# First-batch attention scores as one full-float32 product, and the last short unit's first layer moved between the last tile's layers

## Chip, cores and metric

The kernel runs on one core of a Trainium2 chip. The metric is the device time of one execution in microseconds; for the kernel before, three runs gave 1084.39 us in the median (1082.83 to 1085.16). One further execution was recorded by the hardware profiler; all rows of the trace below are from that one.

## The reference

Causal attention with a decay, over 8 batches of 8 heads (576 positions, 64 wide), then a two-layer feed-forward network (512 to 2048 to 512) over the 4608 rows that it gives. Cut to what matters:

```python
scores = (q @ k.T) / sqrt(64)                       # q, k: (8, 8, 576, 64) float32
cum    = cumsum(log(clip(f, 1e-4, 1)), axis=-1)
scores = where(causal, -1e9, scores + cum[:, None] - cum[None, :])
attn   = softmax(scores)
x      = (attn @ v) -> (4608, 512)
h      = x @ w_in
g      = h * clip(h + 3, 0, 6) / 6
out    = g @ w_out
```

## The kernel before, in words

**Attention, by visits.** The list `VH` (line 97) holds 68 visits. The first batch is cut in another way than the rest: four visits of kind A, each with the first 256 positions of a pair of heads, and eight of kind B, each with the other 320 queries of one head against all 576 keys. Then come 56 visits of kind F, one for each head of the batches 1 to 7. A and B go through `scores` (line 542), which makes scores with the keys on the partitions, so that their exponentials are the weights of the product with v; F goes through `rows` (line 592), which is left as it is apart from its tiles.

**How a product of q and k is made exact.** `load_x` brings q and k of a visit into a tile ST (q on partitions 0 to 63, k on 64 to 127). `parts` (line 442, on GpSimd) rounds them to the reduced type float32r into TQ and TK. `rests` (line 450) copies these rounded parts by two DMAs within the chip into the halves of two further tiles, T7 and T1, and has GpSimd subtract them from ST, so that T7 and T1 also hold what the rounding left. In `group` (line 547) two matmuls then add up in PSUM: line 549 multiplies the rounded parts (with rows for the decay and for the row's maximum, 97 partitions in all), line 550 the mixed products (128 partitions). A third, of float16 and 128 or 64 columns (line 552), adds the causal mask where a block lies on the diagonal. A visit A has four groups (256, 128, 256, 128 columns), a visit B five (320, 320, 320, 192, 64).

**The maximum.** Before that, `natural` (line 475) makes the same scores roughly, from the rounded parts alone, with the queries on the partitions; VectorE takes each row's maximum (line 491); `max_rows` (line 496) turns the maxima by a matmul (line 500), and a DMA of SyncE (line 503) lays them as row 96 of TQ. The names of this chain in the profile are `pn`, `MC`, `ptm` and `mr`.

**Buffers.** TQ and TK have three buffers (visit v uses v mod 3), T1 and T7 two, ST three. So `parts` of a visit waits until the `scores` three visits before have read TK and TQ; `load_x` waits until `rests` has read ST; and the DMAs of `rests` wait until the `scores` two visits before have read T1 and T7.

**Weights.** w_in and w_out come as 64-bit floats, in 32 pieces of 512 KB. Each is loaded (line 238) into one of a few slots, turned into float32 by one instruction of ScalarE and two of VectorE (lines 251 to 253), squared on ScalarE for its scale (line 257), and split in two float16 halves (`w_split`, lines 284 to 295: for most of w_in by two matmuls, lines 287 and 288; for the last quarter of w_in and all of w_out by VectorE, line 295). `W_RATE` hands out eight such steps in a visit A, two in a visit B and four in a visit F.

**The network, as filler.** Once a batch's rows are there, `moe_tile` works off 512 of them: 16 first-layer units (`h_unit`, line 768, matmuls of lines 775 to 777, then ScalarE, VectorE, ScalarE, VectorE into gT) and four second-layer units (`out_unit`, line 815, 48 matmuls of 512 columns each, lines 819 to 821, into a PSUM tile `po`, one eviction by ScalarE, line 825, one DMA). The 64 rows of a batch that are left over go pairwise through `moe_short` (line 848): four `h_short` units (48 matmuls of 128 columns each, lines 797 to 799, into `phs`) and one `out_unit`. These units are generators; `fill` (line 917) puts pieces of them between the steps of the visits. The PSUM tiles of these units come from `mm_tile` (line 761): every third from `ps_t` (one buffer), the others from `ps_m` (two buffers).

**Order.** A scheduler then orders each engine's instructions by its own estimate of when each can start. Each engine and SyncE's queue of DMAs runs its instructions strictly in that order.

**The end.** After the last visit nothing is left but the last tile and the last short unit: first layer of the tile, its second layer, first layer of the short unit (whose result goes into the first 128 columns of gT, which the second layer has read by then), second layer of the short unit.

Of the kernel before, what the change touches and what calls it, by code (L numbers as in the profile page):

```python
# [20 lines left out]
def kernel(  # L21
# [87 lines left out]
    TQ = [cpool.tile([97, SP], F32R, name=f"TQ{i}") for i in range(NQK)]  # L109
    TK = [cpool.tile([97, SP], F32R, name=f"TK{i}") for i in range(NQK)]  # L110
    T1 = [cpool.tile([P, SP], F32R, name=f"T1{i}") for i in range(NL)]
    T7 = [cpool.tile([P, S], F32R, name=f"T7{i}") for i in range(NL)]
# [5 lines left out]
    def init_qk(i, eng):  # L118
        eng.memset(TQ[i].bitcast(F32)[64:96, :], 0.0)
        eng.memset(TQ[i].bitcast(F32)[64:66, :], 1.0)  # L120
        eng.memset(TK[i].bitcast(F32)[64:96, :], -1.0)
        eng.memset(TK[i].bitcast(F32)[96:97, :], 1.0)
        eng.memset(TK[i].bitcast(F32)[:, S:], 0.0)

# [289 lines left out]
    def load_c(v):  # L414
        kind, n = VH[v]
        t = TK[v % NQK].bitcast(F32)[D:D + 2]
# [9 lines left out]
        else:  # L426
# [4 lines left out]
            if PIN0:  # L431
                small.append(d.ins)

# [16 lines left out]
    def rests(v):  # L450
        i, j = v % NQK, v % NL
        s = ST[v % NST]
# [43 lines left out]
    def max_rows(v):  # L496
        i = v % NQK
# [5 lines left out]
        d = nc.sync.dma_start(TQ[i].bitcast(F32)[96:97, 0:m * P], mr.bitcast(F32)[:m])  # L503
# [38 lines left out]
    def scores(v):  # L542

        i, j = v % NQK, v % NL
        ph = p2.tile([P, 1600], F32, tag="PHL", name=f"pf_{v}")

        def group(dst, k0, q0, q1, m):
            ks = slice(k0, k0 + P)
            nc.tensor.matmul(dst, TK[i][0:97, ks], TQ[i][0:97, q0:q1], start=True, stop=False)
            nc.tensor.matmul(dst, T1[j][:, ks], T7[j][:, q0:q1], start=False, stop=(m == 0))  # L550
# [238 lines left out]
    def h_short(u, j):  # L789
# [20 lines left out]
        g = [gT[:, i, n * j:n * j + n, 0:P] for i in range(2)]  # L810
# [4 lines left out]
    def out_unit(s, three, col, rows_):  # L815
        po = mm_tile(f"po_{rows_[0]}", three)
        ts_ = slice(s * P, (s + 1) * P)
        for fc in range(NFC):
            nc.tensor.matmul(po, gT[:, 0, fc, ts_], w2[:, fc, 0, :], start=(fc == 0), stop=False)  # L819
            nc.tensor.matmul(po, gT[:, 0, fc, ts_], w2[:, fc, 1, :], start=False, stop=False)  # L820
            nc.tensor.matmul(po, gT[:, 1, fc, ts_], w2[:, fc, 0, :], start=False, stop=(fc == NFC - 1))  # L821
            if fc % 2 and fc < NFC - 1:
                yield 2.0 - H_COST
# [7 lines left out]
    def moe_tile(t, c0=0, c1=TT):  # L831
# [10 lines left out]
        if c0 == 0:  # L842
            moe_scale_out(t)
# [217 lines left out]
```

## Time and profile before

| | us |
|---|---|
| three runs, median (lowest to highest) | 1084.39 (1082.83 to 1085.16) |
| the profiled execution's own time | 1078.21 |
| its span, first to last instruction | 1076.4 |
| TensorE busy | 1012.2 (94% of the span), 7650 matmul records |
| VectorE busy | 731.5 (68%) |
| ScalarE busy | 587.9 (55%) |
| GpSimd busy | 407.8 (38%) |
| mean granted TensorE clock | 0.989 |

How to read the trace: PE is TensorE, DVE VectorE, ACT ScalarE, POOL GpSimd, SP SyncE (SPq its DMA queue). A matmul's record lasts from its start to the modelled end of its results, so records of a stream overlap; what one costs in a stream is the distance from its start to the next one's. A matmul with full float32 operands shows as two records, one with any other type as one. "Idle before, releaser" names what ended an engine's idle time.

### The profile page before, as it was taken

The page shows a single profiled execution, that of the slowest core. Times are in us where ns is not written, and L with a number is a line of the kernel's source. Part 1 is how long each engine was busy: PE and PEld are TensorE (multiplying, and loading weights), DVE is VectorE, ACT ScalarE, POOL GpSimd, SP SyncE. Part 2 cuts the span into 40 slices and gives each one's busy share as a digit, 9 for nine tenths or more (in the row PEclk, how much of TensorE's full clock was granted, in tenths as well). Part 3 has the DMA queues.
Part 4 walks back from the last instruction along what each step waited for, and adds up shares of the span by engine and source line. Part 5 has one row for each costly group of instructions (what it writes and reads, how often), then busy time and mean ns, then how long its engine had stood idle before and what let it go on. Part 6 is the DMA issues. An engine that isn't in the chain of part 4 may idle for free.

```text
span 1076.4 us, 21155 instructions
## 1 busy us (share of the span) xinstructions
PE 1012.2 (94%) x7650; PEld 600.5 (56%) x7650; DVE 731.5 (68%) x1903; ACT 587.9 (55%) x1189; POOL 407.8 (38%) x505
## 2 busy tenths in 40 slices
PE   2889987899999999999999999999999999999995
PEld 1557854665555755555555755555555755544453
DVE  7897999996885669866865677767855678305101
ACT  4787656765664557555654557555744567225102
POOL 7353455454433444443434344543442442000000
PEclk9989989999999999999999999999999999999999
DMA  7976548966656766567465476557565654300010
GB/s 241 288 212 191 135 100 149 201 146 128 156 101 137 138 151 129 114 148 162 97 127 109 104 167 128 127 133 170 106 110 113 118 96 86 70 30 1 1 40 10
DMA packets 259140, 133.78 MB, mean 124 GB/s; under 512 B 226933, under 2 KB 228525, under 8 KB 259037
## 3 DMA queue, kind: packets, MB, share of 16 engines
q1 hardware_dynamic: 259036, 132.44, 55.6%
q8 instruction: 60, 0.98, 0.4%
q14 instruction: 44, 0.35, 0.1%
HBM read 47.93 MB, written 9.73 MB: 54 GB/s over the span
## 4 chain that ended last, share of the span: by engine, by line
PE 65%; DVE 17%; ACT 6%; issue 5%; DMA 5%; SPq 1%; POOL 1%; ACTq 0%; DVEq 0%; POOLq 0%
PE po L819 10%; PE po L821 10%; PE po L820 10%; PE ph L775 7%; PE ph L776 6%; PE ph L777 6%; DVE pp L620 3%; PE pn L609 3%; PE pn L612 3%; ACT pp L632 2%; DVE ring L649 2%; DMA vst<-in_vS_dram 2%; DVE gT L786 2%; DVE r L784 1%; DVE nb L626 1%
## 5 line engine op out<-in xcount | busy, mean ns | idle before, releaser
L820 PE MATMUL po<-w,gT 128*128 128x512 f16 x576 | 215.7, 382 | 2.5 <-DVE w L295 2.5
L819 PE MATMUL po<-w,gT 128*128 128x512 f16 x576 | 213.6, 382 | 4.1 <-ACT gT L811 3.1
L821 PE MATMUL po<-w,gT 128*128 128x512 f16 x576 | 215.7, 382 | 0.1
L632 ACT ACTIVATE pp<-pp,nb 128x192 f32<-128x192 f32 x280 | 138.9, 552 | 134.8 <-DVE nb L626 134.2
L775 PE MATMUL ph<-xT,w 128*128 128x512 f16 (+1 forms) x576 | 200.2, 358 | 7.1 <-DVE r L784 6.9
L649 DVE TENSOR_TENSOR ring<-pp,ring 128x128 f16<-128x128 f32 (+2 forms) x216 | 144.5, 678 | 83.6 <-ACT ring L646 80.8
L776 PE MATMUL ph<-xT,w 128*128 128x512 f16 (+1 forms) x576 | 199.7, 357 | 0.0
L777 PE MATMUL ph<-xT,w 128*128 128x512 f16 (+1 forms) x576 | 199.2, 357 | 0.0
L447 POOL TENSOR_SCALAR TK<-ST 64x576 fp32r<-64x576 f32 (+1 forms) x68 | 50.1, 737 | 245.2 <-PE pn L609 202.5
L620 DVE CUSTOM_DVE_ANT_0 pp<-pn,W 128x192 f32<-128x192 f32 x280 | 123.3, 482 | 24.7 <-PE pn L612 22.5
L459 POOL TENSOR_TENSOR T<-ST,T 64x576 fp32r<-64x576 f32 (+1 forms) x68 | 99.7, 1466 | 82.8 <-DMA T<-TK 74.3
L609 PE MATMUL pn<-TK,TQ 68*128 68x192 f32 x336 | 124.4, 384 | 6.3 <-issue 5.2
L784 DVE SCALAR_TENSOR_TENSOR r<-r,ph 128x512 f32<-128x512 f32 (+1 forms) x144 | 89.1, 620 | 54.6 <-ACT r L781 54.2
L785 ACT CAST gT<-r 128x512 f16<-128x512 f32 (+1 forms) x144 | 81.5, 569 | 76.9 <-DVE r L784 76.2
L786 DVE TENSOR_TENSOR gT<-r,gT 128x512 f16<-128x512 f32 (+1 forms) x144 | 102.8, 717 | 20.6 <-ACT gT L785 19.0
L781 ACT ACTIVATE r<-ph,bias_r,SC 128x512 f32<-128x512 f32 (+1 forms) x144 | 103.6, 724 | 20.7 <-PE ph L777 17.5
L646 ACT CAST ring<-pp 128x192 f16<-128x192 f32 x280 | 114.3, 449 | 0.0
L612 PE MATMUL pn<-T,T 128*128 128x192 f32 x336 | 113.0, 363 | 0.0
L456 POOL TENSOR_TENSOR T<-ST,TQ 64x576 fp32r<-64x576 f32 (+2 forms) x68 | 100.2, 1474 | 14.2 <-PE pn L612 5.3
L821 PEld LDWEIGHTS <-gT 128*128 128x128 f16 x576 | 56.5, 99 | 71.1 <-issue 9.4
L820 PEld LDWEIGHTS <-gT 128*128 128x128 f16 x576 | 56.5, 99 | 63.4 <-issue 6.4
L655 POOL TENSOR_TENSOR ring<-pp,ring 128x128 f16<-128x128 f32 x96 | 59.9, 624 | 78.2 <-ACT ring L646 33.9
(146 smaller groups left out, 1958.0 us busy)
## 6 DMA issues: line engine op xcount, KB each, us to landing
ST<-in_qk_dram SPq DMA_DIRECT2D x64, 288.0 KB
T<-TK SPq DMA_DIRECT2D x64, 144.0 KB
out_dram<-o SPq DMA_DIRECT2D x33, 256.0 KB
ring<-in_w_out_dram SPq DMA_DIRECT2D x16, 512.0 KB
T<-TQ SPq DMA_DIRECT2D x56, 144.0 KB
vst<-in_vS_dram SPq DMA_DIRECT2D x7, 1040.0 KB
ring<-in_w_in_dram SPq DMA_DIRECT2D x9, 512.0 KB
w<-in_w_in_dram SPq DMA_DIRECT2D x7, 512.0 KB
```

The lines of the kernel that those rows point to most:

```text
L609: nc.tensor.matmul(dst, TQ[i][0:D + 4, qs], TK[i][0:D + 4, a:e], start=True, stop=False)
L612: nc.tensor.matmul(dst, T7[j][:, qs], T1[j][:, a:e], start=False, stop=True)
L620: nc.vector.tensor_tensor_reduce(pp[:r, w:w + kw], pn[:r, o:o + kw], W[:r, 4 * P + r - kw:4 * P + r], 1.0, -3.0e38, ALU.add, ALU.max, accu ...
L632: nc.scalar.activation(x_, x_, AF.Exp, bias=nb[:r, e0 + x:e0 + x + 1], scale=0.125)
L649: eng.tensor_tensor(hl[:r, a:a + c * P], pp[:r, at[c] + 64:at[c] + kw], hl[:r, h0[c] + 64:h0[c] + kw], op=ALU.subtract,)
L775: nc.tensor.matmul(ph, w1[0][:, cc, fs_], xh, start=(cc == 0), stop=False)
L776: nc.tensor.matmul(ph, w1[0][:, cc, fs_], xl, start=False, stop=False)
L777: nc.tensor.matmul(ph, w1[1][:, cc, fs_], xh, start=False, stop=(cc == NCC - 1))
L786: nc.vector.tensor_tensor(gT[:, 1, fc, c0:c1], r, gT[:, 0, fc, c0:c1], op=ALU.subtract)
L819: nc.tensor.matmul(po, gT[:, 0, fc, ts_], w2[:, fc, 0, :], start=(fc == 0), stop=False)
L820: nc.tensor.matmul(po, gT[:, 0, fc, ts_], w2[:, fc, 1, :], start=False, stop=False)
L821: nc.tensor.matmul(po, gT[:, 1, fc, ts_], w2[:, fc, 0, :], start=False, stop=(fc == NFC - 1))
```

## The change

Two independent edits.

**Scores of the visits A and B.** `group` issues one matmul with full float32 operands on 97 partitions in the place of the two float32r ones: `T1[...][0:97]` by `T7[...][0:97]`, which now hold k and q as they are. The mask's matmul stays. A new `load_raw` brings q and k for these two tiles straight from HBM (two DMAs a visit) and the decay rows a second time (`load_c(v, raw=True)`: one or two small DMAs); `rests` does only that for A and B, so the two copies within the chip and GpSimd's two subtractions are gone for these 12 visits. `init_raw` sets the constant rows of the two tiles once. The maxima go to row 96 of T7, no longer of TQ. `natural` and `parts` stay. TQ and TK are now only read by `natural` in these visits, and shrink to 68 partitions. T1 and T7 come from a pool of their own, since F takes them as float32r tiles.

**The end.** The last tile and the last short unit become one generator: first layer of the tile, then the short unit's four `h_short` units into a buffer of their own (`gs`, in the tile vst, which is free by then), then the tile's four second-layer units, then the short unit's second layer as two `out_unit`s of 256 columns each, with an eviction and two DMAs each.

```diff
     def rests(v):
+        if VH[v][0] != "F":
+            load_raw(v)
+            return
         i, j = v % NQK, v % NL
+        T1[j] = p_r.tile([P, SP], F32R, tag="T1", name=f"T1_{v}")
+        T7[j] = p_r.tile([P, S], F32R, tag="T7", name=f"T7_{v}")
...
+    def load_raw(v):
+        kind, n = VH[v]
+        nq, nk, q0 = spans(v)
+        load_c(v, raw=True)
+        for t, d, o, w in ((T7, 0, q0, nq), (T1, D, 0, nk)):
+            t = t[v % NL][0:D, 0:w]
+            if kind == "A":
+                nc.sync.dma_start(
+                    t.rearrange("p (h s) -> p h s", h=2),
+                    qk[2 * n:2 * n + 2, d:d + D, 0:QA].rearrange("h p s -> p h s"),
+                )
+            else:
+                nc.sync.dma_start(t, qk[n, d:d + D, o:o + w])
...
-        d = nc.sync.dma_start(TQ[i].bitcast(F32)[96:97, 0:m * P], mr.bitcast(F32)[:m])
+        d = nc.sync.dma_start(T7[v % NL][96:97, 0:m * P], mr.bitcast(F32)[:m])
...
         def group(dst, k0, q0, q1, m):
-            ks = slice(k0, k0 + P)
-            nc.tensor.matmul(dst, TK[i][0:97, ks], TQ[i][0:97, q0:q1], start=True, stop=False)
-            nc.tensor.matmul(dst, T1[j][:, ks], T7[j][:, q0:q1], start=False, stop=(m == 0))
+            nc.tensor.matmul(
+                dst, tk[0:97, k0:k0 + P], tq[0:97, q0:q1], start=True, stop=(m == 0)
+            )
...
+        last = t == B - 1
+        if last:
+            gs = vst.bitcast(F16).rearrange("p c e -> p (c e)")[:, 0:2 * NFC * P]
+            gs = gs.rearrange("p (a f t) -> p a f t", a=2, f=NFC)
+            for j in range(NG):
+                yield from h_short(t // 2, j, gs)
         r0 = t * S + (64 if t else 0)
         for s in range(c0 // P, c1 // P):
             yield from out_unit(s, t > 0 or s * P >= QA, UO + t, [r0 + s * P])
+        if last:
+            for cols in ((0, DM // 2), (DM // 2, DM)):
+                yield from out_unit(0, True, UX + t, [(t - 1) * S, t * S], gs, cols)
...
+    init_raw(0, nc.gpsimd)
+    rests(0)
...
-            if b % 2:
+            if b % 2 and b < B - 1:
                 queue(moe_short(b // 2), P)
```

**How the order moves, first place: SyncE's queue near its start.** The names are the destinations; `mr` is the row of maxima of a visit, `w` and `ring` are slots for weights, `Q` and `K` the new names of T7 and T1. Before, from the first visit's maxima to the second's:

```order
L503 DMA TQ_93<-mr_187 1x4x128
L355 DMA v_111<-in_vS_dram 128x3x520
L356 DMA xT_118<-in_vS_dram 128x520
L357 DMA xT_118<-in_vS_dram 64x520
L407 DMA ST_103<-in_qk_dram 128x2x256
L238 DMA ring_126<-in_w_in_dram 128x1024
L412 DMA ST_104<-in_qk_dram 128x576
L238 DMA w_115<-in_w_in_dram 128x1024
L422 DMA TK_96<-decay_dram 2x2x256
L454 DMA T_101<-TQ_95 64x512
L455 DMA T_99<-TK_98 64x512
L503 DMA TQ_94<-mr_246 1x4x128
```

Now, the same stretch and the row behind it:

```order
L525 DMA Q_104<-mr_196 1x4x128
L359 DMA v_114<-in_vS_dram 128x3x520
L360 DMA xT_121<-in_vS_dram 128x520
L361 DMA xT_121<-in_vS_dram 64x520
L416 DMA ST_108<-in_qk_dram 128x576
L422 DMA TK_97<-decay_dram 2x576
L416 DMA ST_106<-in_qk_dram 128x576
L525 DMA Q_105<-mr_244 1x4x128
L242 DMA w_118<-in_w_in_dram 128x1024
```

Two weight pieces and two copies within the chip no longer stand between the two visits' maxima; the next weight piece follows behind both.

**Second place: VectorE where the visits B end and the visits F begin.** `w_115` and `w_118` with line 295 or 299 are splits of w_out, `pp` is the first step of an F visit's softmax, `pp_0_1670` and `pp_0_1608` that of the first one. Before:

```order
L726 TENSOR_SCALAR rs_0_1642<-rs_0_1642,SC 128x3
L620 ISA pp_0_1670,MF_108<-pn_0_1661,W 128x192
L620 ISA MF_108 128x1
L620 ISA pp_0_1670,MF_108<-pn_0_1661,W 128x576
L620 ISA MF_108 128x1
L620 ISA pp_0_1670,MF_108<-pn_0_1661,W 64x64
L620 ISA MF_108 64x1
L387 COPY SC<-SC 64x1
L727 TENSOR_TENSOR xf_1640<-pav,rs_0_1642 128x3x64
L295 SCALAR_TENSOR_TENSOR w_115<-w_115,SC 128x512
```

Now:

```order
L299 SCALAR_TENSOR_TENSOR w_118<-w_118,SC 128x512
L757 TENSOR_TENSOR xhl_1410<-xf_1409,xhl_1410 128x3x128
L299 SCALAR_TENSOR_TENSOR w_118<-w_118,SC 128x512 x4
L745 TENSOR_SCALAR rs_0_1580<-pav 128x3
L748 RECIPROCAL rs_0_1580<-rs_0_1580 128x3
L750 TENSOR_SCALAR rs_0_1580<-rs_0_1580,SC 128x3
L751 TENSOR_TENSOR xf_1578<-pav,rs_0_1580 128x3x64
L299 SCALAR_TENSOR_TENSOR w_118<-w_118,SC 128x512 x4
L644 ISA pp_0_1608,MF_111<-pn_0_1599,W 128x192
```

Before, all 16 splits of w_out stand behind the first F visit's `pp`, spread over the first six F visits; now ten stand ahead of it and the other six behind it, before the second F visit's `pp`.

**Third place: TensorE at the very end.** Before, the short unit's first layer (`phs_3`) and its second layer (`po_12475`) meet so:

```order
L798 MATMUL phs_3_12420<-xS_120,w_113 128x128
L799 LDWEIGHTS w_114
L799 MATMUL phs_3_12420<-xS_120,w_114 128x128
L819 LDWEIGHTS gT
L819 MATMUL po_12475<-w_115,gT 128x512
```

Now the end of `phs_3` lies between the first 36 matmuls of the first half (`po_0_12523`) and the second half (`po_256_12576`), which is free to start without the last quarter of `gs`:

```order
L847 MATMUL po_0_12523<-w_118,vst 128x256
L821 LDWEIGHTS w_116
L821 MATMUL phs_3_12260<-xS_123,w_116 128x128
L822 LDWEIGHTS w_116
L822 MATMUL phs_3_12260<-xS_123,w_116 128x128
L823 LDWEIGHTS w_117
L823 MATMUL phs_3_12260<-xS_123,w_117 128x128
L845 LDWEIGHTS vst
L845 MATMUL po_256_12576<-w_118,vst 128x256
```

Behind `phs_3` there now come 25 matmuls of `po_256_12576` before the first that needs its result. By the count in `mm_tile`, `phs_0`, `phs_2`, `phs_3`, the tile's second and third second-layer units and both halves share the two buffers of `ps_m`; `phs_1` and the tile's first and fourth unit take the one of `ps_t`.

More of the change, by code (lines that the diff above doesn't have):

```diff
@@ L108 @@
     PIN_V = 1
[L109 to L112, printed above, removed]
+    TQ = [cpool.tile([D + 4, SP], F32R, name=f"TQ{i}") for i in range(NQK)]
+    TK = [cpool.tile([D + 4, SP], F32R, name=f"TK{i}") for i in range(NQK)]
+    p_r = ctx.enter_context(tc.tile_pool(name="p_r", bufs=NL))
+    T1 = [p_r.tile([P, SP], F32, tag="T1", name=f"K1{i}") for i in range(NL)]
+    T7 = [p_r.tile([P, S], F32, tag="T7", name=f"Q7{i}") for i in range(NL)]
     ST = [cpool.tile([P, S], F32, name=f"ST{i}") for i in range(NST)]
@@ L118, in init_qk, with init_raw @@
     def init_qk(i, eng):
[L119 to L123, printed above, removed]
+        eng.memset(TQ[i].bitcast(F32)[64:68, :], 1.0)
+        eng.memset(TK[i].bitcast(F32)[64:68, :], -1.0)
+    def init_raw(j, eng):
+        eng.memset(T7[j][64:96, :], 0.0)
+        eng.memset(T7[j][64:66, :], 1.0)
+        eng.memset(T1[j][64:96, :], 0.0)
+        eng.memset(T1[j][96:97, :], 1.0)
     NAV = 96
@@ L412, in load_x, with load_c @@
             nc.sync.dma_start(t, qk[n])
-    def load_c(v):
+    def load_c(v, raw=False):
         kind, n = VH[v]
-        t = TK[v % NQK].bitcast(F32)[D:D + 2]
+        t = (T1[v % NL] if raw else TK[v % NQK].bitcast(F32))[D:D + 2]
         if kind != "A":
@@ L787, in h_unit, with h_short @@
         yield H_COST
-    def h_short(u, j):
+    def h_short(u, j, gd):
         x = xS[u % 2]
@@ L809, in h_short @@
         nc.vector.scalar_tensor_tensor(r, r, 6.0 * CG, ph, op0=ALU.min, op1=ALU.mult)
-        g = [gT[:, i, n * j:n * j + n, 0:P] for i in range(2)]
+        g = [gd[:, i, n * j:n * j + n, 0:P] for i in range(2)]
         nc.scalar.copy(g[0], r)
@@ L846, in moe_tile @@
             yield from out_unit(s, t > 0 or s * P >= QA, UO + t, [r0 + s * P])
+        if last:
+            for cols in ((0, DM // 2), (DM // 2, DM)):
+                yield from out_unit(0, True, UX + t, [(t - 1) * S, t * S], gs, cols)
     def moe_short(u):
         for j in range(NG):
-            yield from h_short(u, j)
+            yield from h_short(u, j, gT)
         a, b = 2 * u, 2 * u + 1
@@ L939, in done @@
         if h == H - 1:
-            queue(one(b, QA if b == 0 else 0, TT), TT - QA if b == 0 else TT)
-            if b % 2:
+            queue(
+                one(b, QA if b == 0 else 0, TT),
+                TT - QA if b == 0 else TT + P if b == B - 1 else TT,
+            )
+            if b % 2 and b < B - 1:
                 queue(moe_short(b // 2), P)
```

26 lines of the change are left out of this document (14 added, 12 removed).

## Prediction

> **What bounds the kernel now.** I read the busy time by stages first: weights with the A visits (20 to 62 us), the B visits (to 140), the first F visits (to 225), the long middle, the end. After each bracketed count comes the next engine: PE, PEld, DVE, ACT, POOL, then the granted clock and the DMA share.
>
> ```profile
> 20.00:62.00 42.00, 32.30 (x128) 22.43 (x128) 34.62 (x107) 29.62 (x62) 18.18 (x18) 0.96 0.93 283
> 62.00:140.00 78.00, 74.24 (x556) 60.13 (x556) 66.43 (x200) 54.14 (x114) 33.17 (x35) 0.98 0.58 164
> 140.00:225.00 85.00, 68.34 (x610) 48.01 (x609) 81.85 (x211) 54.90 (x120) 47.97 (x47) 0.92 0.79 158
> 225.00:950.00 725.00, 719.94 (x5684) 410.56 (x5684) 506.51 (x1311) 407.31 (x828) 290.51 (x374) 1.00 0.60 123
> 950.00:1076.40 126.40, 114.70 (x671) 57.35 (x669) 27.09 (x40) 32.94 (x51) 0.00 (x0) 0.99 0.05 16
> ```
>
> From 225 to 950 TensorE idles 5 us of 725: it is the bound there, the change leaves that work alone, and I cost it at nothing. So the result is made in the other rows. At 20 to 62 the DMA engines are 93% taken and TensorE idles 9.7 us; at 62 to 140 TensorE idles only 3.8 us of 78; at 140 to 225 VectorE is 96% busy and TensorE idles 16.7 us. TensorE's waits, in the third stage and at the end, come next (total, times, longest):
>
> ```profile
> PE pav L692 <- DMA pT<-ring: 5.0, 4, 2.2
> PE po L820 <- DVE w L295: 2.5, 3, 1.9
> ...
> PE phs L797 <- DVE rs L809: 3.3, 1, 3.3
> PE po L819 <- ACT gT L811: 2.5, 1, 2.5
> PE po L819 <- ACT o L825: 0.8, 1, 0.8
> ```
>
> In the third stage, VectorE's w_out splits hold second-layer matmuls up directly, and its softmax work stands ahead of the transposes (`pT`).
>
> **B visits: the price of full float32.** No full-float32 score matmul is in the trace, but products of two float32 operands are (line 287 with 512 columns, line 703 with 96). TensorE's timeline gives the distances, in B visits and, in the first row, in an A visit's surroundings:
>
> ```profile
> 41.29 2.07 PE L287 MATMUL low<-gT,eye 128*128 128x512 f32 x2
> ...
> 82.97 1.02 PE L287 MATMUL low<-gT,eye 128*128 128x512 f32 x2
> 83.83 0.38 PE L288 MATMUL low<-w,ident 128*128 128x512 f16 x1
> 84.05 1.47 PE L703 MATMUL pav<-v,pf 128*128 128x96 f32 x12
> 85.36 0.39 PE L703 MATMUL pav<-xT,pf 128*128 128x96 f32 x2
> ...
> 131.40 0.31 PE L549 MATMUL ps<-TQ,TK 97*128 97x320 f32 x1
> 131.54 0.31 PE L550 MATMUL ps<-T,T 128*128 128x320 f32 x1
> 131.70 0.32 PE L549 MATMUL ps<-TQ,TK 97*128 97x320 f32 x1
> ...
> 132.04 0.34 PE L549 MATMUL ps<-TQ,TK 97*128 97x192 f32 x1
> ...
> 132.37 0.28 PE L549 MATMUL ps<-TQ,TK 97*128 97x64 f32 x1
> ```
>
> One full-float32 product of 512 columns takes 83.83 - 82.97 = 0.86 us. So 320 columns take 0.54 (by columns), against 0.30 for the pair now (131.40 to 131.70): +0.24. For few columns each record takes at least (85.36 - 84.05)/12 = 0.11. The 192-column group takes 0.33 now (132.04 to 132.37) with its 0.07 of mask, 0.26 without, and 0.32 then: +0.06; the 64-column one has two records of 0.11 either way: nothing. A B visit: 3 x 0.24 + 0.06 = +0.78; eight: +6.2 us, in a stage whose 3.8 us of idle could hide as much at best: +2.4 to +6.2, and up to +7.5 if the operands' 97 rows load worse than the rows quoted. I take +5: of the waits, the one for GpSimd's TQ goes, 1.4 us in this stage, and it most likely has no heir, since `parts` then waits for no scores.
>
> ```profile
> PE pn L485 <- POOL TQ L448: 1.4, 1, 1.4
> ```
>
> The Trainium skill ("FP8 and Floating Point Precision", TensorE Precision Notes) says that true float32 goes through the array four times. Four passes against two would double each pair: 2 x 1216 columns at 0.15 a 320 are 1.14 us more a visit, 9.1 for eight; the trace agrees for wide groups and not for the narrow ones, which it shows already held by something else.
>
> **A visits and the loads.** An A visit has two groups of 256 columns (+0.19 each, scaled from the 320) and two of 128 (none): +0.4, twice that where the array runs at half rate as at 41.29 (2.07 against 1.02 for the same two records). Four visits: +1.6 to +3.2 us, beside 9.7 us of idle; I count them as hidden. If that cover goes, they are paid in full. Against that stands the wait for the maxima (`mr`), here for the second visit:
>
> ```profile
> 25.68 0.35 PE L500 MATMUL ptm<-identr,MC 128*4 128x128 f32 x1
> ...
> 26.73 0.33 SPq L238 DMA_DIRECT2D w<-in_w_in_dram  x1
> ...
> 28.72 0.67 SPq L503 DMA_DIRECT2D TQ<-mr  x1
> ...
> 34.90 0.55 PE L549 MATMUL ps<-TQ,TK 97*128 97x256 f32 x1 [3.12 <-DMA TQ<-mr]
> ```
>
> The maxima are turned at 25.68, but SyncE reaches their DMA only at 28.72, behind a weight load that had to wait for its slot and the copies within the chip; the 2 KB then land 6 us later behind those loads. In the new order nothing but the loads of v, two loads of q and k and one of the decay stand between the first visit's maxima and the second's, and TensorE turns the second's before the first's scores. So the second visit's scores should start some 5 us earlier. What is late next is the third visit's maxima: six weight pieces, and the raw loads of the third and fourth visit, which wait for the scores of the first and second, stand ahead of them on SyncE's queue. SyncE also issues one or two decay loads more a visit; at 0.33 to 0.67 us an issue (rows above) that is some 8 us over 120, on a queue that waits for slots anyway, and I cost it at nothing. The bytes are the same (the raw loads replace copies of their size), and at 93% the DMA engines allow at most 42 x 0.07 = 3 us by bytes alone. I take -3.3 for the stage, between -8 (all of the 9.7 us but the float32) and +2 (no wait gone, two thirds of the upper 3.2 paid).
>
> GpSimd and VectorE bear on this stage and the next:
>
> ```profile
> L459 POOL TENSOR_TENSOR T<-ST,T x13: 1258/1406/1837, 18.4 to 130.2; 64x576 fp32r<-64x576 f32 x9, 64x512 fp32r<-64x512 f32 x4
> POOL TK L447 <- PE ps L549: 16.2, 5, 6.3
> ...
> L252 DVE TENSOR_SCALAR gT<-gT 128x512 int32<-128x512 int32 x16 | 10.3, 642 | 5.3 <-ACT gT L251 5.3
> L252 DVE TENSOR_SCALAR w<-w 128x512 int32<-128x512 int32 x16 | 8.4, 524 | 5.5 <-ACT w L251 5.5
> ...
> 75.31 0.41 DVE L252 TENSOR_SCALAR w<-w 128x512 int32<-128x512 int32 x1
> ...
> 76.28 1.44 POOL L459 TENSOR_TENSOR T<-ST,T 64x576 fp32r<-64x576 f32 x1 [3.23 <-DMA T<-TK]
> ...
> 76.40 1.60 DVE L252 TENSOR_SCALAR w<-w 128x512 int32<-128x512 int32 x1
> ```
>
> Of GpSimd's subtractions, 24 go, at 1.4 us (the row has the twelve of one kind and one of an F visit; I take the other kind as alike); `parts` no longer waits for scores (16.2 us). Line 252 takes 0.41 us alone and 1.60 beside such a subtraction: its 32 runs took 18.7 us instead of 32 x 0.41 = 13.1, so VectorE lost up to 5.6 us there. It idles in these stages, so I count none of it as time; as a rival I do. The Trainium skill ("GPSIMD Engine Reference", 1. Specifications) says that GpSimd shares VectorE's SBUF interfaces and contends with its 2-port modes; by that rule the 24 x 1.4 = 34 us could all hold VectorE up. The trace agrees in kind, with 5.6 us in this line.
>
> **First F visits.** The splits of w_out lie here now:
>
> ```profile
> L295 DVE SCALAR_TENSOR_TENSOR w<-w,SC x16: 732/740/1447, 140.2 to 194.2; 128x512 f16<-128x512 f32 x16
> ```
>
> Ten of the 16 move ahead of the first F visit's softmax, into the end of the B visits, where TensorE is the bound and VectorE idles 78 - 66.4 = 11.6 us. 10 x 0.74 = 7.4 us leave a stage that VectorE bounds, and second-layer matmuls, free to run, fill TensorE meanwhile. Against it: what doesn't fit before delays the first softmax. I take -4, between -9 (with the GpSimd stalls of these splits, up to 1447 ns) and +2.
>
> **The end.** ScalarE's and VectorE's steps, then the last eviction and its DMAs:
>
> ```profile
> 1051.92 2.84 ACT L805 ACTIVATE rs<-phs,bias_r,SC 128x256 f32<-128x256 f32 x6 [6.58 <-PE phs L799]
> 1053.88 1.88 DVE L809 SCALAR_TENSOR_TENSOR rs<-rs,phs 128x512 f32<-128x512 f32 x3 [49.39 <-ACT rs L805]
> ...
> 1065.86 1.02 ACT L805 ACTIVATE rs<-phs,bias_r,SC 128x256 f32<-128x256 f32 x2 [9.45 <-PE phs L799]
> 1066.91 0.69 DVE L809 SCALAR_TENSOR_TENSOR rs<-rs,phs 128x512 f32<-128x512 f32 x1 [9.35 <-ACT rs L805]
> ...
> 1071.41 0.69 ACT L825 ACTIVATE o<-po,SC 128x512 f32<-128x512 f32 x1 [3.15 <-PE po L821]
> 1072.12 1.15 SPq L828 DMA_DIRECT2D out_dram<-o  x2
> ```
>
> The three waits quoted first make 6.6 us. They don't all go. After the first three `phs` all three PSUM buffers still hang on ScalarE and VectorE: the next unit waits for the first step of VectorE instead of the second, 3.3 - 0.7 = 2.6 us. At the last `phs` the 25 matmuls put behind it cover gT's delay, but `po_256` needs the buffer of `phs_3` itself: 1.02 + 0.69, with handovers some 1.9 us. The 0.8 goes. So 4.5 of 6.6 stay: -2.1. Two halves in place of one unit cost TensorE nothing if 256 columns take half of 512; the last eviction gets shorter, but SyncE has four DMAs of 1.15/2 = 0.58 to issue instead of two, so I cost the tail behind it at nothing. The tiles that F now takes from a pool of their own have the same two buffers and readers: nothing either. Bounds: -4 (the buffers come free earlier) to +0.5.
>
> **Sum.** -3.3 + 5 - 4 - 2.1 = -4.4 us on the profiled execution's 1078.2, which is 6.2 below the median of the runs; on the median 1084.4 it gives 1080.0.
>
> **Rivals.** (1) Slower: TensorE is the bound from the A visits on. It pays 6.2 + 1.6 for full float32, neither loads nor splits give anything, only the end gains: +7.8 - 2.1 = +5.7, 1090.1. For: 3.8 us of idle in 78. Against: idle on both sides of that stage. It decides from the point where the first B visit's scores start no earlier than now and the third stage stays as long; the chain of waits has that start:
>
> ```profile
> 60.76 0.15 PE ps L549
> ```
>
> (2) No change: the splits ahead of the first softmax delay it by as much as they spare: -0.4, 1084.0. For: VectorE's order is strict. (3) VectorE, freed of GpSimd, carries the front: another 5.6 us, 1074.4. For: the 1.60 us row. Against: VectorE idles in those stages. This is the rule from "GPSIMD Engine Reference" of the Trainium skill at work. (4) That the float32 matmul isn't done in full passes: the 0.86 us row speaks against it; no chance of its own.
>
> **Numbers.** Forecast 0.44 (1076.5 to 1082.2 by itself), rival 1 0.22, rival 2 0.22, rival 3 0.12. About 0.2% (2.2 us) is what a measurement of this kernel can tell from no change. Faster 0.56, same 0.22, slower 0.22. The range 1073 to 1089 takes in the forecast, rival 2, most of rival 3 and the milder half of rival 1.
>
> **What would show it.** Right: score records of 320 columns in pairs 0.27 us apart; B visits 0.6 us longer each; the second visit's scores near 30 us, not 34.9; the first B scores at 57 to 58, not 60.8; line 299 largely done before the first `pp`, TensorE's idle between 140 and 225 down by 4; at the end waits of 2.6 and 1.9 in place of 3.3, 2.5 and 0.8. Wrong: score records at the old distance, a third stage as long as now, or `po_256` not waiting for VectorE.

## The result and the profile after

The change made the kernel slower: 1097.15 us (median of 4 runs, 1094.24 to 1104.44) against 1084.78 before (4 runs), a ratio of 1.0126 with a 95% interval of 1.0082 to 1.0171, or +13.7 us. The forecast was 1080.0, faster; the result lies above the whole range. The profiled execution of the changed kernel took 1094.24 us, its span 1092.5, against 1078.21 and 1076.4 before: +16.

The windows of the changed kernel, in the columns of the prediction's first fence:

```profile
20.00:62.00 42.00, 26.77 (x106) 18.92 (x107) 27.55 (x98) 26.63 (x57) 8.04 (x10) 0.90 0.92 289
62.00:140.00 78.00, 76.05 (x477) 56.52 (x476) 51.90 (x163) 50.85 (x107) 10.47 (x17) 0.90 0.51 152
140.00:225.00 85.00, 78.55 (x628) 58.26 (x626) 70.11 (x201) 54.02 (x113) 36.32 (x35) 0.94 0.54 106
225.00:300.00 75.00, 65.84 (x555) 38.06 (x555) 61.85 (x183) 48.21 (x104) 42.61 (x48) 0.98 0.84 172
300.00:950.00 650.00, 643.42 (x5134) 367.86 (x5133) 457.25 (x1182) 366.28 (x740) 262.39 (x340) 1.00 0.61 125
```

The stretch from 225 to 300 us was part of a long row in the prediction; alone, before, it is:

```profile
225.00:300.00 75.00, 73.25 (x571) 42.23 (x571) 60.73 (x159) 48.64 (x104) 33.29 (x42) 1.00 0.65 139
```

Read TensorE's busy time and its granted clock together. In the A visits TensorE idles 15.2 us instead of 9.7. In the B visits it idles less than before (2 us of 78), but at a clock of 0.90 instead of 0.98: 76.05 x 0.10 = 7.6 us of its time went to the lower clock, against 74.24 x 0.02 = 1.5. In the third stage it idles 6.5 us instead of 16.7, as if the forecast's gain had come; but behind it, from 225 to 300, it idles 9.2 us where it had idled 1.8. From 300 us on the two kernels run alike.

When the first F visit, and the fifteenth, start their first product gives the same story as a delay. Before, in TensorE's timeline:

```profile
137.39 0.36 PE L609 MATMUL pn<-TK,TQ 68*128 68x192 f32 x1
...
313.95 0.44 PE L609 MATMUL pn<-TK,TQ 68*128 68x192 f32 x1
```

The changed kernel:

```profile
162.46 0.44 PE L633 MATMUL pn<-TK,TQ 68*128 68x192 f32 x1
...
329.88 0.44 PE L633 MATMUL pn<-TK,TQ 68*128 68x192 f32 x1
```

The first F visit is 25.1 us late, the fifteenth 15.9, and so are all later ones to within 1 us, down to the span's end (+16.1). Part of the 25 us was no loss: second-layer matmuls had been moved ahead of the first F visit. The 15.9 are the loss, and all of it was made in the first 300 us.

How it begins shows in the first A visit. TensorE's timeline before, and then SyncE's, GpSimd's and TensorE's rows in the changed kernel:

```profile
12.21 1.38 PE L485 MATMUL pn<-TK,TQ 66*128 66x128 f32 x4 [12.21 <-DMA TK<-cs]
...
23.20 0.58 PE L549 MATMUL ps<-TQ,TK 97*128 97x256 f32 x1 [4.90 <-DMA TQ<-mr]
```

```profile
13.67 1.45 SPq L432 DMA_DIRECT2D K<-cs  x2
...
21.66 0.66 SPq L525 DMA_DIRECT2D Q<-mr  x1
...
12.24 0.69 POOL L466 TENSOR_SCALAR TQ<-ST 64x512 fp32r<-64x512 f32 x1
...
15.22 0.61 POOL L466 TENSOR_SCALAR TQ<-ST 64x512 fp32r<-64x512 f32 x1
...
15.88 2.38 PE L508 MATMUL pn<-TK,TQ 66*128 66x128 f32 x8 [15.88 <-POOL TQ L466]
...
26.30 1.22 PE L572 MATMUL ps<-Q,K 97*128 97x256 f32 x2 [5.42 <-DMA Q<-mr]
27.32 0.31 PE L576 MATMUL ps<-ident,W 128*128 128x128 f16 x1
```

The products for the first maxima start 3.7 us late and the first scores 3.1. GpSimd clears the raw tiles first, but that does not decide: its copies for this visit are done at 12.93, and the copy that ends at 15.83, which the row of 15.88 names, is the second visit's. What comes late is this visit's first decay row. SyncE issues it at 10.11 us (10.25 before), and by the trace's semaphores it lands at 15.74 instead of 12.07. The raw loads of the first two visits now go out ahead of it, and the DMA engines are still full where they had room (their busy share is the last number but one; before, then now):

```profile
11.00:13.00 2.00, 0.79 (x3) 0.72 (x4) 1.97 (x4) 1.52 (x4) 1.83 (x4) 1.00 0.18 64
```

```profile
11.00:13.00 2.00, 0.00 (x0) 0.00 (x0) 1.62 (x3) 1.87 (x6) 1.85 (x4) 1.00 1.11 213
```

Then the maxima's DMA goes out at 21.66 us instead of 19.35, behind the second visit's two raw decay rows (0.72 us each) and five issues more. The third visit shows how such a delay is passed on, in the timelines of TensorE, ScalarE and VectorE:

```profile
45.48 0.67 PE L572 MATMUL ps<-Q,K 97*128 97x256 f32 x2 [1.23 <-DMA Q<-mr]
...
48.78 0.68 ACT L255 ACTIVATE gT<-w 128x512 f32<-128x512 f32 x1 [4.09 <-DMA w<-in_w_in_dram]
...
51.72 0.66 ACT L255 ACTIVATE gT<-ring 128x512 f32<-128x512 f32 x1 [0.87 <-DMA ring<-in_w_in_dram]
...
52.90 0.88 ACT L592 ACTIVATE pf<-ps,bias_p 128x768 f32<-128x768 f32 x1
...
53.48 0.27 DVE L524 TENSOR_SCALAR mr<-ptm 4x128 fp32r<-4x128 f32 x1
```

The scores are made by 47.4 us, but their exponential (line 592) stands behind two weight steps (line 255) in ScalarE's order, and these wait for pieces of the first layer still on their way; VectorE's maxima for the next visit stand behind the same pieces' shifts. So the exponential comes at 52.90 instead of 47.04. TensorE's waits from 20 to 62 us say the same from the other side (total, times, longest):

```profile
PE ps L572 <- DMA Q<-mr: 7.4, 3, 5.4
PE ptm L522 <- DVE MC L514: 4.5, 2, 3.0
PE pn L508 <- ACT pf L592: 1.8, 1, 1.8
```

Two parts of the change could be at fault: what it does (float32, loads, clearing), and the order that the planner laid out for it.

### The profile page after: what moved, and what is told of

It is laid out like the page before. It is cut to its first block, busy times and chain, and to the rows that moved or that the text cites. A ratio compares the mean times of both kernels' runs of the same rounds, so it can differ in the third digit from the quotient of the medians.

```text
span 1092.5 us, 21228 instructions
## 1 busy us (share of the span) xinstructions
PE 1026.3 (94%) x7698; PEld 611.8 (56%) x7698; DVE 709.7 (65%) x1903; ACT 589.1 (54%) x1190; POOL 375.4 (34%) x480
## 4 chain that ended last, share of the span: by engine, by line
PE 56%; DVE 9%; ACT 6%; issue 4%; DMA 3%; POOL 1%; SPq 1%; ACTq 0%; DVEq 0%; POOLq 0%
PE po L845 9%; PE po L847 9%; PE po L846 9%; PE ph L799 6%; PE ph L801 6%; PE ph L800 6%; PE pn L636 2%; PE pn L633 2%; DVE pp L644 2%; ACT pp L656 2%; DVE ring L673 1%; DMA pT<-ring 1%; ACT ring L670 1%; DVE r L808 1%; DVE gT L810 1%
## 5 line engine op out<-in xcount | busy, mean ns | idle before, releaser
L845 PE MATMUL po<-w,gT 128*128 128x512 f16 x560 | 209.1, 382 | 5.3 <-DVE rs L833 2.8
L656 ACT ACTIVATE pp<-pp,nb 128x192 f32<-128x192 f32 x280 | 138.5, 552 | 137.1 <-DVE nb L650 135.2
L847 PE MATMUL po<-w,gT 128*128 128x512 f16 x560 | 209.6, 382 | 0.0
L846 PE MATMUL po<-w,gT 128*128 128x512 f16 x560 | 209.6, 382 | 0.0
L810 DVE TENSOR_TENSOR gT<-r,gT 128x512 f16<-128x512 f32 (+1 forms) x144 | 100.1, 699 | 18.5 <-ACT gT L809 17.4
L482 POOL TENSOR_TENSOR T<-ST,T 64x576 fp32r<-64x576 f32 x56 | 82.2, 1467 | 67.7 <-DMA T<-TK 52.5
L847 PEld LDWEIGHTS <-gT 128*128 128x128 f16 x560 | 54.9, 99 | 66.0 <-issue 7.4
L846 PEld LDWEIGHTS <-gT 128*128 128x128 f16 x560 | 54.9, 99 | 64.7 <-issue 9.6
L479 POOL TENSOR_TENSOR T<-ST,TQ 64x576 fp32r<-64x576 f32 x56 | 83.8, 1496 | 21.1 <-issue 8.6
L801 PEld LDWEIGHTS <-w 128*128 128x128 f16 x576 | 56.7, 99 | 56.6 <-issue 6.4
```

Source lines behind the costliest of these rows:

```text
L656: nc.scalar.activation(x_, x_, AF.Exp, bias=nb[:r, e0 + x:e0 + x + 1], scale=0.125)
L801: nc.tensor.matmul(ph, w1[1][:, cc, fs_], xh, start=False, stop=(cc == NCC - 1))
L845: nc.tensor.matmul(po, g[:, 0, fc, ts_], w2[:, fc, 0, c], start=(fc == 0), stop=False)
L846: nc.tensor.matmul(po, g[:, 0, fc, ts_], w2[:, fc, 1, c], start=False, stop=False)
L847: nc.tensor.matmul(po, g[:, 1, fc, ts_], w2[:, fc, 0, c], start=False, stop=(fc == NFC - 1))
```

## The experiments

All ratios are to the kernel before, run on the same chip; the microseconds are (ratio - 1) times its median there (1079.9 to 1081.4).

**One half of the change at a time.** Four kernels. The end alone is the kernel before with the change's hunks of `h_short`, `out_unit`, `moe_tile` and `queue`, and the scores alone are the changed kernel without them. A alone and B alone keep the old end and the old path beside the new one, and choose by the kind of visit, with `RAW` naming the kinds; the edit to the changed kernel, cut to its core:

```diff
-        if VH[v][0] != "F":
+        if VH[v][0] in RAW:
             load_raw(v)
             return
...
-            nc.tensor.matmul(
-                dst, tk[0:97, k0:k0 + P], tq[0:97, q0:q1], start=True, stop=(m == 0)
-            )
+            if VH[v][0] in RAW:
+                nc.tensor.matmul(
+                    dst, tk[0:97, k0:k0 + P], tq[0:97, q0:q1], start=True, stop=(m == 0)
+                )
+            else:
+                nc.tensor.matmul(dst, TK[i][0:97, ks], TQ[i][0:97, q0:q1], start=True, stop=False)
+                nc.tensor.matmul(dst, tk[:, ks], tq[:, q0:q1], start=False, stop=(m == 0))
```

The expectations set two theories of what the change does against each other. One ("TensorE", later "passes") says that the added time of TensorE is what is paid; the other ("queue", later "set-up") blames the raw loads, the decay rows and the clearing at the start. The end alone, expected:

> The kernel before with the second half of the change alone: the last short unit's first layer between the last tile's layers, its output in two halves. Both theories: the front is untouched, so only the end can move. The trace of the changed kernel has 2.8 and 1.8 us of waits at the end where before had 3.3, 2.5 and 0.8, but 5.0 us instead of 4.3 from the last output DMA's issue to the end: -0.8 to -2.1 us, 1082.7 to 1084.0. If it is slower than before, the end has a share in the loss that neither theory has.

Measured 1078.04 us, ratio 0.9978 (0.9963 to 0.9993): -2.4 us. TensorE's waits at its end are those of the changed kernel, 2.8 and 1.8 us:

```profile
PE po L821 <- DVE rs L809: 4.6, 2, 2.8
```

The scores alone:

> The changed kernel with the old end, so the full-float32 scores alone. Both theories put the whole loss here: +13 to +17 us, 1098 to 1102, and the first F visit's scores some 25 us later than before (162 us instead of 137). If it comes out under +10, the end has a share.

Measured 1103.69, ratio 1.0213 (1.0162 to 1.0264): +23.0, the whole loss and more than was expected; its first F visit starts at 169 us. Its order up to the end is the changed kernel's; the two differ by 9.3 where the end explains 2.4, within what both intervals leave open.

The A visits alone, then the B visits alone:

> Old end; full float32 on raw q and k in the four A visits alone, the B visits as before. Theory TensorE (the added passes sit on a TensorE that bounds the A and B visits, at half clock after its gaps): the A visits have 16 of the 56 score matmuls and under a fifth of the columns, so +1 to +4 us. Theory queue (the raw and decay loads change SyncE's order, so that the maxima of the third and fourth visit and weight pieces of the first layer go out 2 to 8 us later, and ScalarE and VectorE, whose order is strict, hold the exponentials up behind the late weight pieces): the queue is upset in just these visits, +8 to +14 us.

> Old end; full float32 on raw q and k in the eight B visits alone, the A visits as before. Theory TensorE: four fifths of the added work is here, +6 to +12 us. Theory queue: the A visits' loads and weight pieces stand as before, so -2 to +4 us. If the two runs of one half each don't add up to the run of both, the halves act on each other through the order of the instructions.

Measured: A alone 1.0112 (1.0063 to 1.0162), +12.1; B alone 0.9999 (0.9976 to 1.0022), -0.1. Theory TensorE, which put four fifths of the float32 into the B visits, seemed to fall: the stage with most of the added work cost nothing. But what "A alone" changes is work, loads, clearing and order at once.

**Passes without loads, and the set-up undone.** The first kernel is the one before with two more passes of a tile of zeros per score group in the A visits. The others ease the set-up of the raw tiles:

```diff
+            for x in range(2 if VH[v][0] == "A" else 0):
+                nc.tensor.matmul(
+                    dst, Z, TQ[i][0:64, q0:q1], start=False, stop=(m == 0 and x == 1)
+                )
...
-    init_raw(0, nc.gpsimd)
+    init_raw(0, nc.vector)
...
-                nc.sync.dma_start(
+                (nc.scalar if v < 2 else nc.sync).dma_start(
                     t.rearrange("p (h s) -> p h s", h=2),
```

The second hunk stands for all the clearing of the raw tiles, the third also for their decay rows.

> The kernel before, with two more float32r passes of a tile of zeros behind each score group of the four A visits, so that TensorE does as many passes there as with full float32, and nothing of the loads changes. Theory passes (the +12 us of the run with full float32 in the A visits alone are TensorE's, at half clock behind its gaps): +8 to +14 us. Theory set-up (the raw loads and decay loads on SyncE's queue and the clearing of the raw tiles on GpSimd put the first visit 3 us and weight pieces five and six 5 us late, and the strict orders pass that on): -1 to +3 us.

Measured 1.0100 (1.0067 to 1.0133), +10.8: with no load added. But the zeros were dearer than meant. In TensorE's timeline, the first A visit of a later kernel with the same zeros (before's order):

```profile
22.94 0.58 PE L552 MATMUL ps<-TQ,TK 97*128 97x256 f32 x1 [5.04 <-DMA TQ<-mr]
23.32 0.42 PE L553 MATMUL ps<-T,T 128*128 128x256 f32 x1
23.67 0.79 PE L555 MATMUL ps<-TQ,Z 64*128 64x256 f32 x2
24.40 0.29 PE L559 MATMUL ps<-ident,W 128*128 128x128 f16 x1
```

To its mask the group takes 24.40 - 22.94 = 1.46 us; full float32 takes 27.32 - 26.30 = 1.02 (rows above), and the old pair 0.60. So the zeros add 0.86 where full float32 adds 0.42 (and for 128 columns, where full float32 adds 0.06, they add 0.7). The runs with zeros are a test of whether TensorE's time is paid, not its price.

> Full float32 in the A visits alone, old end, with the raw tiles cleared on VectorE instead of GpSimd. GpSimd's first rounded copy should start near 9.8 us as before, not at 12.5, and the first maxima come 2 to 3 us earlier. Theory passes: as the run without this edit, +9 to +14 us over before. Theory set-up: the queue's part is left, +5 to +10 us.

Measured 1.0034 (1.0009 to 1.0059), +3.7. This looked like a win for the set-up theory, but the trace says otherwise. GpSimd's copies do start at 9.2 us; but a load that waited held SyncE up, so the maxima and scores of the first visit came later than in any kernel here (SyncE's and TensorE's timelines):

```profile
27.93 0.66 SPq L541 DMA_DIRECT2D Q<-mr  x1
...
30.58 1.22 PE L589 MATMUL ps<-Q,K 97*128 97x256 f32 x2 [1.22 <-DMA Q<-mr]
```

A first visit 7.4 us later than before, and yet only +3.7 at the end: how late the first visit is does not decide alone (the order was another one here too).

> As the run with the clearing on VectorE, and the first two visits' raw q, k and decay loads are issued by ScalarE instead of SyncE: weight pieces five and six should go out by 17 us again (19.6 and 20.5 with the loads on SyncE), the first maxima by 19 us. Theory set-up: +0 to +5 us over before. Theory passes: +9 to +14 us. A third outcome, +5 to +9, would say that the later visits' loads, which still are on SyncE, carry the rest.

Measured 1.0087 (1.0056 to 1.0119), +9.4, worse than without the edit, and the step that was to bring the gain did not happen: pieces five and six went out at 20.88 and 24.95, not by 17.

> The changed kernel itself (all A and B visits in full float32, new end) with the same two edits: raw tiles cleared on VectorE, the first two visits' raw and decay loads issued by ScalarE. Theory set-up: the B visits cost nothing and the end gives 2.4, so -3 to +3 us of before. Theory passes: +8 to +13 us, as the changed kernel.

Measured 1.0074 (1.0051 to 1.0098), +8.0 for the whole change, at the lower edge of what the passes would give and far from the set-up's. Neither of the two edits worked as it was meant to, and each kernel had been laid out anew by the planner. That made the order itself the suspect.

**The order held.** Edges that set the issue order alone, and add no wait, tie each engine's instructions to the order of another kernel:

```diff
+        queue = []
+        for k in seq:
+            queue.append(own[k])
+            queue += behind.get(own[k].name, [])
+        for a, b in zip(queue, queue[1:]):
+            tc.add_manual_dep(b, a.name, dep, reason="as in the other kernel")
```

`seq` has the other kernel's order of an engine's instructions by their place in the program, `own` this kernel's instructions, and what is added (`behind`) follows its neighbour at once.

Zeros in the A visits, in the order before; then the order that came with those zeros, without the zeros; then full float32 in all visits, in the order before; then zeros in all visits, in the order before:

> The kernel before with the two passes of zeros behind the score groups of the A visits, as in the run without new loads, but with every engine's instructions (SyncE's DMAs among them) held in the order of the kernel before. The passes had come with another order: the planner, which lays the order out by times of its own, saw dearer scores. Theory order (the re-laid order costs, the passes themselves only their 2.6 us at full clock or 5 at half): +1 to +5 us. Theory passes: +8 to +13 us, as with the free order (+10.8).

> The kernel before, nothing added or taken away, with every engine's instructions held in the order that the planner had laid out for the kernel with the passes of zeros in the A visits. Theory order: +5 to +11 us. Theory passes: -1 to +2 us.

> Full float32 on raw q and k in all twelve visits, old end, with TensorE's, VectorE's and ScalarE's instructions held in the order of the kernel before (each score group's two matmuls become one); SyncE and GpSimd are left to the planner, since their instructions differ. With its free order the same program took +23 us. Theory order: +0 to +8 us. Theory passes or set-up: +12 to +23 us, since passes, loads and clearing are all there.

> As the first of these with two passes of zeros behind the score groups of all twelve visits, every engine held in the order of the kernel before. This prices full float32's passes where nothing else moves: 12 visits at 0.27 us a group of 320 columns make 8 to 9 us at full clock. If TensorE bounds these stages, +7 to +14 us; if it has slack, +2 to +6 us.

Measured: +9.8 (1.0091, 1.0066 to 1.0116); +6.5 (1.0060, 1.0030 to 1.0089); +7.5 (1.0069, 1.0041 to 1.0098); +19.6 (1.0181, 1.0121 to 1.0241). So both theories hold a part. Passes are paid: with the zeros the four A visits' scores take TensorE 5.5, 5.5, 4.2 and 3.3 us in the timeline, where they took 2.5, 2.4, 2.7 and 1.3. That is 9.5 us more, and 9.8 were paid. And an order costs, with nothing added: +6.5. Full float32, at +7.5 in the old order, is a third of its +23 in its own.

**The changed kernel's own order, priced.** The kernel before in the order laid out for the full-float32 scores; the changed kernel, complete, in the order of the new end alone; B alone and A alone in the order before:

> The kernel before, nothing added, taken away or loaded otherwise, with TensorE's, VectorE's and ScalarE's instructions held in the order that the planner laid out for full float32 in all twelve visits (old end). Theory two parts (the added passes are paid one for one, some 7 us, and the re-laid order costs about as much again or more): +5 to +14 us. Theory passes alone: -2 to +2 us.

> The changed kernel, nothing left out, with TensorE's, VectorE's and ScalarE's instructions held in the order of the kernel with the new end alone. Theory two parts: the run of the scores in the order before took +7.5, the new end alone -2.4, so +3 to +8 us, some 8 less than the changed kernel in its own order. Theory passes alone: +10 to +15 us, as the changed kernel.

> Full float32 in the eight B visits alone, old end, TensorE, VectorE and ScalarE in the order of the kernel before. In its own order this took +0 us. Theory two parts: TensorE bounds these visits and pays the added passes, 8 visits at 0.5 to 0.8 us, +3 to +7 us, and the free order had been a lucky one. If the B visits have room for the passes (or GpSimd's relief pays for them), -2 to +2 us.

> Full float32 in the four A visits alone, old end, TensorE, VectorE and ScalarE in the order of the kernel before. In its own order this took +12 us. Theory two parts: the passes at half clock cost 1 us a visit and the first visit comes some 3 us late behind the clearing and the loads, of which the gaps that follow take some back: +2 to +6 us, and with the B visits' run it should make up the +7.5 of both. Theory set-up alone: +8 to +12 us, whatever the order.

In these four SyncE's and GpSimd's instructions are the planner's own to place, so that "order" includes what it made of them. The first decides: with nothing added, the order alone takes 1.0126 (1.0089 to 1.0162), +13.6 us, as much as the whole change. The second is its counterpart: the complete change in the old order takes 1.0015 (0.9995 to 1.0035), +1.6 us. It has the same kind of edges, so these by themselves don't make the 13.6; the kernel before tied to its own order was not run. B alone takes 1.0027 (1.0003 to 1.0051), +2.9; A alone 1.0066 (1.0041 to 1.0091), +7.1; their sum of 10 agrees with the 7.5 of both within the intervals. The windows of the kernel before in the new order:

```profile
20.00:62.00 42.00, 32.21 (x131) 23.12 (x131) 33.41 (x102) 28.57 (x62) 19.11 (x18) 0.92 0.91 273
62.00:140.00 78.00, 67.16 (x464) 53.26 (x464) 53.78 (x156) 48.82 (x104) 25.07 (x30) 0.91 0.50 151
140.00:225.00 85.00, 76.37 (x621) 56.76 (x622) 70.92 (x216) 55.39 (x120) 37.41 (x39) 0.94 0.55 110
225.00:300.00 75.00, 65.30 (x554) 40.45 (x553) 60.72 (x168) 44.80 (x96) 42.30 (x48) 0.95 0.81 171
```

They are the changed kernel's: the clock of 0.91 in the B visits, 9.7 us of idle behind 225. Only its B visits idle more (10.8 us), where the changed kernel had float32 to fill the time. Added up over the four rows, TensorE idles 39.0 us where it idled 31.9, and loses 16.5 to the lower clock (busy time times the missing share of the clock) where it lost 8.2. That makes some 15 us, half of it by the clock, and the fifteenth F visit is 14.6 late. What TensorE waits for there and behind 225 in this kernel:

```profile
PE low L288 <- ACT w L290: 2.3, 1, 2.3
PE pn L486 <- issue: 1.9, 2, 1.6
PE ps L550 <- DVE MC L492: 1.2, 1, 1.2
...
PE pav L695 <- DMA pT<-ring: 4.1, 3, 2.3
```

No single wait stands out. Now the complete change in the old order:

```profile
20.00:62.00 42.00, 30.20 (x111) 20.83 (x111) 26.16 (x93) 24.55 (x52) 7.26 (x12) 1.00 0.93 288
62.00:140.00 78.00, 77.81 (x523) 59.54 (x524) 58.56 (x183) 56.77 (x118) 13.91 (x19) 0.98 0.56 162
140.00:225.00 85.00, 69.28 (x607) 48.89 (x606) 80.49 (x227) 55.64 (x121) 45.50 (x43) 0.92 0.76 150
225.00:300.00 75.00, 72.69 (x580) 43.63 (x580) 62.22 (x165) 45.84 (x98) 36.60 (x43) 1.00 0.64 142
```

The B visits are full, at 0.98; behind 225 the idle time is 2.3 us, much as before. The float32 is there, the raw loads and the clearing are there, the first visit's scores start even later (27.16 us), and the loss is gone.

**Which stretch of the order.** Two kernels hold an order only up to the first B visit's scores and leave the rest to the planner: the kernel before with the front of the full-float32 order, and the scores alone with the front of the old one.

> The kernel before, nothing added, with TensorE, VectorE and ScalarE held in the order laid out for full float32 only up to the first B visit's scores (their first matmul, their maxima and the fourth A visit's exponentials); the planner lays out the rest afresh for the program as it is, and puts as little second-layer work ahead of the first F visit as before. Theory front (the +13.6 of that order come from the A visits, where weight steps stand ahead of exponentials and maxima): +8 to +14 us. Theory later (they come from the B and F visits, whose order follows the planner's dear scores): -2 to +4 us.

> Full float32 in all twelve visits, old end, with TensorE, VectorE and ScalarE held in the order of the kernel before up to the same place; the planner lays out the rest for full float32, with the second layer's work ahead of the first F visit again. In its own order throughout this program took +23 us, in the order before throughout +7.5. Theory front: +5 to +10 us. Theory later: +13 to +23 us.

Measured +6.2 (1.0057, 1.0033 to 1.0080) and +22.9 (1.0212, 1.0174 to 1.0251). Neither theory has it alone: the front costs some 6 us, and with the old front the rest, laid out for full float32, still costs the whole +23, 15 more than the same program in the old order throughout. In the windows of the last kernel TensorE has gaps in the third stage and the next; its longest wait in the third stage stands below them:

```profile
140.00:225.00 85.00, 69.34 (x572) 50.81 (x571) 64.56 (x172) 49.06 (x105) 34.95 (x33) 0.90 0.57 120
225.00:300.00 75.00, 68.00 (x569) 41.26 (x569) 65.62 (x182) 49.19 (x108) 42.96 (x50) 0.95 0.82 162
...
PE ph L800 <- DMA xT<-xhl: 9.2, 1, 9.2
```

TensorE idles 15.7 us at a clock of 0.90 and 7.0 at 0.95, and VectorE is no bound in either. The wait of 9.2 us is a first-layer matmul that stands in TensorE's order ahead of the transposed rows that it needs: they are ready at 178.7 us, SyncE issues their transpose only at 183.6, and TensorE starts at 187.2. Where the rest's order puts the second layer can be counted: before, no second-layer matmul of the first tile (`po`) stands ahead of the first F visit's products and 2 ahead of the second's; in the order for full float32 it is 30 and 80, and in the last kernel 42 and 96. TensorE's work is done early there, beside visits that leave little room, and is missing later, when it waits for transposes. That is how I read it; one engine's order with the others as before was not tried, and which rows of the order cost most stays open.

## Why the prediction was wrong

**The step that failed** is the sum itself: it adds the costs of instructions, loads and waits, and takes the order as a few moved rows whose effect can be read at the three places where it was looked at. The order of the first 300 us was another one throughout, and by itself costs 13.6 us (1.0126 in place of 1). Without it the change takes +1.6 (1.0015, -0.5 to +3.8), inside the forecast's range and within what a measurement can tell from no change, but not the -4.4 of the sum: one more term failed, that of the A visits. That the prediction saw ten w_out splits move, and called it a gain, was reading one row of the new order and not the rest. Several signs that it named came true (records 0.27 us apart, the splits ahead of the first `pp`, the two waits at the end), and the kernel still lost: they are signs of single steps, not of the time.

**A visits, forecast -3.3 (bounds -8 to +2).** Wrong in the old order too: +7.1 (4.4 to 9.8). The float32 itself was priced right: in that run the four visits' scores take TensorE 12.0 us where they took 8.9, +3.1 in bounds of 1.6 to 3.2 (a visit 0.96 at half rate, 26.30 to 29.74 against 23.20 to 25.68, and 0.42 at full). But it was counted as hidden in 9.7 us of idle time, and the zeros show that TensorE's time in these visits is paid one for one (9.5 added, 9.8 paid). The idle time lies where TensorE waits for maxima, and a longer score group delays the next exponentials, maxima and weight steps just the same. That leaves some 4 of the 7.1. In the same run the first visit's scores start 4.0 us late (27.23), with the decay rows late as above. The bytes of the raw loads were counted over the whole stage, where they replace others, and not at the place where they now go out first; SyncE's added issues were costed at nothing. That this is all of the rest is not shown. The second visit's scores were to start near 30 us instead of 34.90; in the changed kernel they start at 33.97, behind a first visit that is 3.1 late.

**B visits, forecast +5 (2.4 to 7.5).** In the old order +2.9 (0.3 to 5.5): sign and mechanism held, and so did the prices. Two 320-column groups take 69.89 - 68.81 = 1.08 us in the changed kernel's timeline, 0.54 each, as forecast:

```profile
68.81 1.24 PE L572 MATMUL ps<-Q,K 97*128 97x320 f32 x4
69.89 1.02 PE L291 MATMUL low<-gT,eye 128*128 128x512 f32 x2
```

With 0.09 more for the group of 192 columns and nothing for that of 64, a visit's scores take 0.81 us more at full clock where 0.78 was forecast, some 6.5 for eight. That 2.9 of them are paid is near the lower bound, in which the stage's 3.8 us of idle time cover a part; in that run TensorE's idle time from 62 to 140 us falls to 2.0, so that some of it is covered. The page "FP8 and Floating Point Precision" of the Trainium skill (TensorE Precision Notes) counts four passes for true float32; 0.54 against the 0.30 of a pair comes near four against two, and the 64-column groups, 0.32 with their mask in both kernels, do not follow it.

**First F visits, forecast -4.** Ten of 16 splits did move ahead of the first `pp`, and TensorE's idle time from 140 to 225 fell by 10. That was no gain: from 225 to 300 it rose by 7.4, and the first `pp` came at 166.7 us instead of 138.5. The stage's idle time was not saved but put off, and the splits' share of it was not measured alone.

**The end, forecast -2.1.** Measured -2.4 (-4.0 to -0.8), with waits of 2.8 and 1.8 us where 2.6 and 1.9 were forecast. Right, by the steps given: where the clock stays up, the stretch from the last F visit's first product to the end is 162.4 us with the new end (the complete change in the old order) and 164.7 before. The clock can change that in either kernel. Where it fell behind the first of the waits, the stretch took 164.0 (the end alone) and 168.5 (before, in the new order), so a single execution does not show the gain.

**The rivals.** Rival 1 (TensorE pays for full float32 from the A visits on) had the sign, and its +7.8 for the scores is near what they cost in the old order, +7.5. But that is luck: it had 1.6 in the A visits and 6.2 in the B visits, and alone they cost 7.1 and 2.9. One half of its test held, the first B visit's scores start at 68.8 us, not 60.76; the other did not, since TensorE's idle time in the third stage fell. With the end it gave +5.7, and the kernel lost 13.7. Rival 2 had no room for either cost, and rival 3, VectorE freed of GpSimd, can't be seen as a gain of its own in any run.

The new end alone is the best kernel found: 0.9978 of the kernel before.

## What to carry to other kernels

Where a planner lays out the order, a change that makes an operation dearer in its eyes also re-deals the order of everything near, and that can outweigh the operation: here +13.6 us against +1.6. Price the two apart: hold the old order with the change in, and the new order with the change out. Idle time of an engine in a chain of strict queues is no cover for more work on that engine; look at what the next wait behind it is for.

An order is also luck in both directions: B alone cost 0 in its own order and +2.9 in the old one (intervals that overlap), A alone with VectorE's clearing +3.7 in its own, without it +12.1. A verdict on an edit that was only timed in its own order is a verdict on the pair.

## What the runs showed of the hardware

TensorE's clock, once down, stayed down through full work. In windows of the changed kernel (the last columns are the granted clock, the DMA engines' share and GB/s):

```profile
50.20:53.60 3.40, 1.13 (x8) 0.97 (x8) 1.93 (x5) 2.53 (x6) 0.00 (x0) 1.00 0.97 358
53.50:56.00 2.50, 0.74 (x2) 0.29 (x2) 2.49 (x10) 2.24 (x6) 1.20 (x2) 0.53 1.43 287
...
58.60:67.30 8.70, 8.70 (x21) 5.13 (x22) 5.85 (x21) 6.18 (x14) 0.00 (x0) 0.50 0.70 235
66.00:68.50 2.50, 2.50 (x16) 1.82 (x14) 1.11 (x3) 1.52 (x4) 0.00 (x0) 0.74 0.69 172
```

TensorE ends its work at 52.0 us, and at about 53.6 it is granted half (a mean of 0.53 over the second window); though it works without a gap from 58.6 us it gets the full clock only near 67.3 (a mean of 0.74 over the last). "TensorE: Matmul & The Clock Gate" of the Trainium skill (Part 1) has a window of about 3.4 us for both directions. The trace agrees with neither direction as it stands: in the 3.4 us before the fall TensorE worked for 1.1, and the rise took 67.3 - 58.6 = 8.7 us. Why, no run here shows. And the clock of the profile's rows reads 1.00 at the start, while a 256-column group takes 1.02 us at 26.3 and 0.51 at 45.5: the first visits run at half rate with nothing in that column.
